# Attention in half-chunks of 64 tokens with two states per unit, and joint TensorE groups in one double-bank tile

## The chip, the cores and the metric

The kernel runs on one core of a Trainium2 chip. The metric is the device time of one execution in microseconds. TensorE (PE) does the matmuls, VectorE (DVE), ScalarE (ACT) and GpSimd (POOL) work beside it, and SyncE (SP) issues most transfers. Each engine runs its own instructions in program order and waits for others on semaphores. Matmul results land in PSUM, in banks of 512 f32 per partition, from where DVE or ACT must fetch them.

## What is computed

A linear attention with decay, whose output goes through a squared-ReLU feed-forward network (FFN). The inputs are random; the attention's are f32, the FFN's weights f64.

```python
B, H, S, D = 4, 8, 768, 48                # batch, heads, tokens, head size
state = zeros(B, H, D, D)
for t in range(S):
    y[:, :, t] = r_t @ (state + (u * k_t) v_t^T)
    state = w_t[:, :, :, None] * state + k_t v_t^T      # decay per key channel
x = y.transpose(0, 2, 1, 3).reshape(3072, 384)
h = relu(x @ w_in)                        # w_in 384 x 2048
out = (h * h) @ w_out                     # w_out 2048 x 384
```

## The kernel before

The tokens are cut into NC = 6 chunks of C = 128. A unit is one chunk of one batch entry: 24 units, numbered 4c + b, each with 8 heads in NP = 4 pairs. A pair's two heads lie on partitions 0 to 47 and 64 to 111 (J = 64, HP = 112); Q = 64 is half a chunk. Inside a chunk the decay is folded into the keys and queries by running products (DVE scans, L630, and the steps up to L653), so that a unit needs only matmuls.

A unit of chunks 1 to 5 has these steps on PE, f32 and packed four at a time into quarters of the array:

- scores (L693), keys times queries, into two PSUM tiles `mts`; DVE puts them through the causal mask into two SBUF tiles `Ms` (L696), whose diagonal blocks ACT has filled before (`diag`, L680);
- `past`: the old state times the queries (`inter`, L715), 8 matmuls of 128 columns, and the turned keys (`across`, L720), 4 transposes of the whole array; ACT copies the keys to SBUF (L739);
- `mix`: masked scores times values (`part`, L728), added to the same PSUM, and the outer products of keys and values (`outer`, L747), which DVE adds to the state (L809) and POOL multiplies with the chunk's decay (L812).

Then ACT and DVE write the unit's output as a high and a low part (L789, L790) into `xT`, and SP sends six small transfers per two units that put the fourth head pair in place (L797). In chunk 5 no state is kept, so `across` and `outer` fall away. Chunk 0 has no old state and an order of its own.

All PSUM steps of attention take their tiles from the pool `a`, two banks. The FFN has two banks `hp` and four accumulators `ob`. One FFN step multiplies the weights of 128 hidden columns with a chunk's x (L832, 9 matmuls of 512 columns into an hp bank), squares through L837, L838, L840, L841 (ACT, DVE, ACT, DVE) and multiplies with the second weights (L847, 12 matmuls of 384 columns). Chunk 0 runs its first 6, chunk 1 all 16 steps in two half-width parts (`HALF`), so that they can begin when two units are done. The weights come in 8 groups of 1.5 MB, each of which ACT, DVE and POOL split into two f32r parts.

The order on every engine is made by a planner (`Plan`): each step has a cost, its dependencies, and a rank out of a table (`Ranks`); the planner simulates the engines and writes down the order. A step marked with `mode` is one that packs the array. Where it expects PE to idle early on, it puts filler transposes (L888). SP's order of loads comes from the same tables.

Of the kernel before, what the change touches and what calls it, by code (L numbers as in the profile page):

```python
# [35 lines left out]
class Plan:  # L36
# [949 lines left out]
```

## Time and profile before

| | before |
|---|---|
| three runs, us | 546.95, 547.07, 545.52 (median 546.95) |
| profiled execution, its own time | 545.76 us |
| its span | 543.9 us |
| granted TensorE clock | 0.996 |
| PE busy | 526.4 us (97%) |
| DVE / ACT / POOL busy | 367.1 / 281.8 / 101.4 us |

The span runs from the first to the last instruction; the execution's own time is 1.9 us longer. A busy PE is not a PE at its peak, since matmuls overlap: how long a step holds PE is read from one step's start to the next step's start. In a row, `a<-pt,S` says that a tile a was written from pt and S; `x32` counts rows, and an f32 matmul has two rows, an FFN matmul (f32r) and a transpose one.

### The profile page before, as it was taken

Reading aid. Unit: us, or ns where it says so; the run is one execution under the profiler, and the core shown is the slowest. Engines: PE = TensorE matmul, PEld = TensorE weight load, DVE = VectorE, ACT = ScalarE, POOL = GpSimd, SP = SyncE. Lnnn points to the kernel's source line nnn. Section 1 sums busy time; section 2 is a strip of 40 time slices with the busy share of each in tenths; the row PEclk is TensorE's granted clock in tenths of the full one; section 3 lists DMA queues with packets and bytes.
Section 4 is the critical chain, followed back from the end, with each engine's and each line's share of the span. In section 5 each row is a group of like instructions: output and inputs, shape, how many; then the busy total and the mean of one; then the engine's idle time right before and its main releaser. Section 6 shows DMA issues by size and latency. Waiting matters only on the chain.

```text
span 543.9 us, 12917 instructions
## 1 busy us (share of the span) xinstructions
PE 526.4 (97%) x5047; PEld 465.7 (86%) x5047; DVE 367.1 (67%) x770; ACT 281.8 (52%) x730; POOL 101.4 (19%) x121
## 2 busy tenths in 40 slices
PE   8899989999999999999999999999999999999995
PEld 8788978878999889988888888889888989899894
DVE  6889899989969596498859597875653233433331
ACT  3668568486664747356465757526433222432321
POOL 5344543144303021030301203020000000000000
PEclk9999999999999999999999999999999999999998
DMA  9979988666483745747256565644002000000001
GB/s 161 175 183 227 244 173 195 151 109 136 93 151 72 138 91 101 140 92 134 48 97 122 101 125 117 129 91 84 1 6 68 16 1 1 29 32 0 1 1 61
DMA packets 222978, 53.01 MB, mean 97 GB/s; under 512 B 212672, under 2 KB 217792, under 8 KB 222912
## 3 DMA queue, kind: packets, MB, share of 16 engines
q1 hardware_dynamic: 220016, 50.75, 46.6%
q10 hardware_dynamic: 2896, 1.38, 1.0%
q8 instruction: 42, 0.69, 0.6%
q14 instruction: 24, 0.20, 0.1%
HBM read 31.65 MB, written 4.72 MB: 67 GB/s over the span
## 4 chain that ended last, share of the span: by engine, by line
PE 77%; DMA 10%; DVE 4%; ACT 3%; SPq 3%; issue 1%; POOL 0%; ACTq 0%; DVEq 0%
PE hp L832 33%; PE ob L847 32%; DMA ri<-in_moe_w_in_dram 4%; DMA v<-in_v_dram 3%; PE a L693 3%; PE a L728 3%; DMA st<-in_w_dram 2%; PE a L715 2%; SPq L572 2%; PE a L720 1%; PE a L747 1%; ACT m L680 1%; SPq L605 1%; DVE g L841 1%; DVE pt L630 1%
## 5 line engine op out<-in xcount | busy, mean ns | idle before, releaser
L847 PE MATMUL ob<-wo,g 128*128 128x384 f32 x1152 | 223.4, 340 | 1.4 <-DVE g L841 1.4
L832 PE MATMUL hp<-x,wi 128*128 128x512 f32 (+1 forms) x1062 | 219.9, 355 | 3.4 <-DVE g L841 3.2
L847 PEld LDWEIGHTS ob<-wo,g 128*128 128x128 f32 x1152 | 198.9, 188 | 7.7 <-DVE g L841 2.2
L832 PEld LDWEIGHTS hp<-x,wi 128*128 128x128 f32 x1062 | 173.1, 188 | 32.8 <-DVE g L841 6.8
L838 DVE SCALAR_TENSOR_TENSOR hp<-hp,t 128x512 f32<-128x512 f32 (+1 forms) x118 | 69.8, 593 | 91.3 <-ACT t L837 90.8
L837 ACT ACTIVATE t<-hp 128x512 f32<-128x512 f32 (+1 forms) x118 | 61.1, 518 | 118.5 <-PE hp L832 64.2
L841 DVE TENSOR_TENSOR g<-hp,g 128x512 fp32r<-128x512 f32 (+1 forms) x118 | 68.9, 585 | 32.3 <-ACT g L840 31.6
L840 ACT CAST g<-hp 128x512 fp32r<-128x512 f32 (+1 forms) x118 | 59.7, 506 | 51.9 <-DVE hp L838 51.5
L680 ACT ACTIVATE m<-diag,beta 128x64 f32<-128x64 f32 x192 | 50.0, 340 | 11.6 <-DVE beta L668 7.3
L660 POOL TENSOR_TENSOR st<-st 128x384 f32<-128x384 f32 x24 | 24.3, 1017 | 65.6 <-DVE st L581 58.4
L630 DVE TENSOR_TENSOR_SCAN pt<-pt,zero 112x128 f32<-112x128 f32 x80 | 29.0, 412 | 1.7 <-DMA st<-in_w_dram 1.7
L790 DVE SCALAR_TENSOR_TENSOR x<-a,x 112x128 fp32r<-112x128 f32 (+2 forms) x68 | 20.2, 329 | 12.2 <-ACT x L789 10.9
L696 DVE COPY_PREDICATED m<-caus,a 128x384 f32<-128x384 uint8 x48 | 25.9, 584 | 3.1 <-PE a L693 2.9
L662 POOL TENSOR_TENSOR st<-st,un 128x384 f32<-128x384 f32 x24 | 27.3, 1141 | 1.6
L581 DVE STREAM_TRANSPOSE st<-st 128x1152 f32<-128x1152 f32 x20 | 27.0, 1361 | 0.0
L728 PEld LDWEIGHTS a<-m,v 64*48 64x48 f32 (+1 forms) x768 | 20.5, 126 | 7.3 <-issue 4.1
L637 ACT ACTIVATE m<-pt 112x512 f32<-112x512 f32 x24 | 15.2, 631 | 22.3 <-DVE pt L630 19.4
L693 PEld LDWEIGHTS a<-pt 48*64 48x64 f32 x768 | 19.2, 133 | 7.8 <-ACT m L680 1.6
L789 ACT ACTIVATE x<-a 112x128 fp32r<-112x128 f32 (+2 forms) x68 | 18.1, 313 | 14.1 <-PE a L747 7.0
L728 PE MATMUL a<-m,v 64*48 64x64 f32 (+3 forms) x768 | 24.8, 250 | 0.4 <-DVE m L696 0.4
L693 PE MATMUL a<-pt 48*64 48x128 f32 (+1 forms) x768 | 22.8, 250 | 1.4 <-DVE pt L653 1.4
L812 POOL TENSOR_TENSOR S<-S,Ec 112x192 f32<-112x192 f32 x16 | 8.1, 508 | 82.8 <-DVE S L809 82.8
(86 smaller groups left out, 441.8 us busy)
## 6 DMA issues: line engine op xcount, KB each, us to landing
pt<-st SPq DMA_DIRECT2D x120, 96.0 KB, 2.3
ro<-in_moe_w_out_dram SPq DMA_DIRECT2D x8, 768.0 KB, 7.4
v<-in_v_dram SPq DMA_DIRECT2D x88, 48.0 KB, 2.5
st<-in_w_dram SPq DMA_DIRECT2D x11, 384.0 KB, 4.4
st<-in_k_dram SPq DMA_DIRECT2D x11, 384.0 KB, 5.7
st<-in_r_dram SPq DMA_DIRECT2D x11, 384.0 KB, 5.7
out_dram<-q SPq DMA_DIRECT2D x20, 192.0 KB, 2.1
ri<-in_moe_w_in_dram SPq DMA_DIRECT2D x8, 384.0 KB, 6.4
```

Source lines behind the costliest of these rows:

```text
L581: V.transpose(out=zt[:, i].rearrange("a t p q i -> a t (p q) i"), in_=sv[:, :, i].rearrange("s t p q x -> s t (p q) x"))
L630: lambda p=p: V.tensor_tensor_scan(out=pt[:, 0, p], data0=src(0)[:, p], data1=zero.broadcast_to([HP, C]), initial=1.0, op0=ALU.mult, op1=A ...
L662: P.add("pool", 0.97, rank("rk"), lambda: G.tensor_tensor(out=rk(), in0=rk(), in1=un.rearrange("s (h d) -> s h d", d=D), op=ALU.mult), w=[ ...
L680: A.activation(Ms[j].tile[:, mo(p, y):mo(p, y) + Q], diag2, AF.Copy, scale=beta.tile[:, i:i + 1])
L693: T.matmul(mts[j].tile[q * Q:q * Q + Q, o:o + C - y * Q], kq[js, g:g + Q], pt[js, 1, 2 * q + p, y * Q:], start=True, stop=True, skip_group ...
L728: T.matmul(spot(p)[to:to + n + D, y * Q:], vt.tile[qs, o - n:o + D], Ms[j].tile[qs, mo(p, y):mo(p, y) + C - y * Q], start=(c == 0 and p == ...
L832: T.matmul(hp.tile[:, 0:n], wi[f][:, wl, kt], xT[:, kt, xl, xs], start=(m == 0), stop=(m == 3 * KT - 1))
L837: P.add("act", 0.49 if full else 0.28, rank("g"), lambda: A.activation(t(), h(), AF.Relu), r=[hp], w=[(g, 1)])
L838: P.add("dve", 0.6 if full else 0.33, rank("g"), lambda: V.scalar_tensor_tensor(out=h(), in0=h(), scalar=0.0, in1=t(), op0=ALU.max, op1=AL ...
L840: P.add("act", 0.48 if full else 0.26, rank("g"), lambda: A.copy(out=hi(), in_=h()), r=[hp], w=[(g, 0)])
L841: P.add("dve", 0.6 if full else 0.33, rank("g"), lambda: V.tensor_tensor(out=lo(), in0=h(), in1=hi().bitcast(F32), op=ALU.subtract), r=[hp ...
L847: T.matmul(obs[b][:, 0:DM], g.tile[0][:, gl, o:o + C], wo[f][:, wl], start=(f == 0 and m == 0), stop=(f == NF - 1 and m == 2))
```

## The change

Chunks 1 to 5 get another attention (chunk 0 keeps its own, with a fixed order of the fetches from one bank).

- The pool `a` is now the two halves of one tile `ab` of 1024 columns. From chunk 1 on both halves belong to a fixed layout: for each head pair 128 columns of output (`Y`) and 128 columns of a zone that holds either outer products or scores.
- Scores, mix and old-state products are computed within halves of 64 tokens. For that a unit has two states: `S[b]` at its start, and `S1` = `S[b]` + outer products of its first half. The second half's queries meet `S1`. `S2` = `S1` + outer products of the second half is decayed by POOL into the next `S[b]`. So the matmuls are 16 of 64 columns each for `inter`, `mix` and `scores`, and 16 of 48 for `outer` (8 in chunk 5).
- The keys are turned earlier, in a step of its own (L717) between FFN matmuls, into a bank of the pool `hp`; one ACT copy of 448 columns takes them.
- PE's packed work is done in two groups per unit. `advance(k)` joins `inter` of unit k with `outer` of unit k + 1, and `mix` of unit k with `scores` of unit k + 1.
- One mask of 512 columns (L780) in place of two of 384; `Ms` becomes one tile `M`; x is fetched in two pieces instead of three; POOL copies the decay in three pieces.
- Keys of the form `(sl, "bank")` put ACT's fetch of x, DVE's mask and DVE's fetch of x in that order.
- All ranks are new, some of the planner's costs differ, and the pool `m` has six tiles instead of seven.

```diff
-    LANES, RUNS, SLACK, START = 8, 2300, 1.0, 3.6
+    LANES, RUNS, SLACK, START = 8, 2300, 1.0, 4.0
     UNITS = (
-        (-1354.91, -1161.61, 40.98, ...
+        (-1377.03, -1144.15, -483.17, ...
-    pas = [ps_a.tile([128, 512], F32, name=f"a{i}") for i in range(2)]
+    ab = ps_a.tile([128, 1024], F32, name="ab")
+    pas = [ab[:, i * 512:i * 512 + 512] for i in range(2)]
+            M, Kt, kp = Slot("m", unit), Slot("m", unit), Slot("hp")
+            P.add("pe", 0.2 * ys, rank("ktp"), turned_k, r=KK, w=[kp])
+            P.add("act", 0.03 + 0.2 * ys, rank("kt"), lambda: A.copy(out=Kt.tile[:, 0:2 * ys * HP], in_=kp.tile[:, 0:2 * ys * HP]), r=[kp], w=[Kt])
+            def outer():
+                for p in range(2):
+                    for y in range(ys):
+                        for j in range(2):
+                            for q in range(2):
...
+            def inter():
+                for h, t in enumerate((lambda: Ss[b], lambda: S1.tile)):
+                    for p1 in range(2):
+                        for j in range(2):
+                            for q in range(2):
+                                p = 2 * q + p1
+                                js, n, to, o = slice(j * J, j * J + D), ahead(p, j), side(p, j) * J, PC + block(p, j) * D
+                                T.matmul(ab[to:to + n + D, p * 2 * C + h * Q:p * 2 * C + h * Q + Q], t()[js, o - n:o + D], pt[js, 1, p, h * Q:h * Q + Q],
+                                         start=(h == 0 and p1 == 0), stop=False, skip_group_check=True)
...
+                P.add("dve", 0.27, rank("S"), lambda: V.tensor_tensor(out=sv(S1.tile), in0=zone(0, D)[0:HP], in1=sv(Ss[b]), op=ALU.add), r=["dS", ("S", b)], w=[S1])
+                    P.add("dve", 0.27, rank("S"), lambda: V.tensor_tensor(out=sv(S2.tile, 0), in0=zone(J, D)[0:HP], in1=sv(S1.tile), op=ALU.add), r=["dS", S1], w=[S2])
+                    P.add("pool", 0.46, rank("S"), lambda: G.tensor_tensor(out=Sd, in0=S2.tile..., in1=Eb(), op=ALU.mult), r=[S2, Ec], w=[("S", b)])
+                P.add("dve", 0.6, rank("mask"), lambda: V.copy_predicated(out=mv(), mask=..., data=zone(0, C)...), r=["scores"], w=[M, ("Y", "bank")])
...
+    def advance(k):
+        a, z = (stages[i] if 0 <= i < len(stages) else None for i in (k, k + 1))
+        if a:
+            fns, r, w, cost = fns + [a["inter"]], r + a["r2"], w + ["Y"], cost + 0.45
+        if z:
+            fns, r, w, cost = fns + [z["outer"]], r + z["r1"], w + ["dS", "scores"], cost + z["outer_cost"]
+        P.add("pe", cost, (a or z)["rank"]("past"), lambda fns=fns: group(fns), r=r, w=w + AB, mode=1, claim=[a["x3"]] if a else [], after=turns)
...
+        if a:
+            fns, r, w, cost = fns + [a["mix"]], r + a["r4"] + ([] if z else ["past"]), w + ["Y"], cost + 0.45
+        if z:
+            fns, r, w, cost = fns + [z["scores"]], r + z["r3"], w + ["dS", "scores"], cost + 0.45
+        P.add("pe", cost, (a or z)["rank"]("mix"), lambda fns=fns: group(fns), r=r, w=w + AB, mode=1, claim=[z["M"]] if z else [])
```

How it moves instructions, at two places. First PE in chunk 1 before the change: the old state's group of one unit, between FFN matmuls (pt are queries and keys, S the state, st and v inputs, m the SBUF tiles of masked scores and keys).

```order
L832 MATMUL hp_146<-x_135,wi_81 128x256 x9
L715 MATMUL a_147<-pt_129,S_132 64x128
L715 MATMUL a_147<-pt_129,S_132 48x128
L715 MATMUL a_148<-pt_129,S_132 48x128
L715 MATMUL a_148<-pt_129,S_132 64x128
L715 MATMUL a_147<-pt_129,S_132 64x128
L715 MATMUL a_147<-pt_129,S_132 48x128
L715 MATMUL a_148<-pt_129,S_132 48x128
L715 MATMUL a_148<-pt_129,S_132 64x128
L720 MATMUL a_147<-ident,pt_129 128x112 x2
L720 MATMUL a_148<-ident,pt_129 128x112 x2
L847 MATMUL ob_141<-wo_79,g_95 128x384 x3
```

After it, PE in chunk 2: the group that joins the two half-chunk products of one unit (with the state S_132 and the middle state S_166) to the outer products of the next one, of which the first two rows are shown:

```order
L742 MATMUL ab<-pt_129,S_132 64x64
L742 MATMUL ab<-pt_129,S_132 48x64 x2
L742 MATMUL ab<-pt_129,S_132 64x64 x2
L742 MATMUL ab<-pt_129,S_132 48x64 x2
L742 MATMUL ab<-pt_129,S_132 64x64
L742 MATMUL ab<-pt_129,S_166 64x64
L742 MATMUL ab<-pt_129,S_166 48x64 x2
L742 MATMUL ab<-pt_129,S_166 64x64 x2
L742 MATMUL ab<-pt_129,S_166 48x64 x2
L742 MATMUL ab<-pt_129,S_166 64x64
L731 MATMUL ab<-v_152,m_159 64x48 x2
L731 MATMUL ab<-v_152,m_159 48x48 x2
```

and, a little later, the group that joins mix and scores:

```order
L936 MATMUL hp_146<-x_136,wi_65 128x512 x9
L761 MATMUL ab<-m_155,v_154 64x64
L761 MATMUL ab<-m_155,v_154 48x64 x2
L761 MATMUL ab<-m_155,v_154 64x64 x2
L761 MATMUL ab<-m_155,v_154 48x64 x2
L761 MATMUL ab<-m_155,v_154 64x64 x2
L761 MATMUL ab<-m_155,v_154 48x64 x2
L761 MATMUL ab<-m_155,v_154 64x64 x2
L761 MATMUL ab<-m_155,v_154 48x64 x2
L761 MATMUL ab<-m_155,v_154 64x64
L751 MATMUL ab<-pt_130 64x64 x16
L936 MATMUL hp_145<-x_136,wi_69 128x512 x9
```

The transposes of the keys (L720, right behind L715) have left the packed group; three visits to the packed array per unit have become two.

The second place is SP near the start, before the change: weight groups 3 and 4 (ri_68, ro_70 and ri_76, ro_78), chunk 1's values v and its raw inputs st.

```order
L519 DMA ri_68<-in_moe_w_in_dram 16x3x512 x2
L521 DMA ro_70<-in_moe_w_out_dram 128x2x768
L605 DMA v_153<-in_v_dram 64x4x48 x4
L605 DMA v_154<-in_v_dram 64x4x48 x4
L572 DMA st_151<-in_w_dram 128x16x48
L572 DMA st_151<-in_k_dram 128x16x48
L572 DMA st_151<-in_r_dram 128x16x48
L519 DMA ri_76<-in_moe_w_in_dram 96x2x512
L519 DMA ri_76<-in_moe_w_in_dram 48x512 x2
L519 DMA ri_76<-in_moe_w_in_dram 16x3x512 x2
L521 DMA ro_78<-in_moe_w_out_dram 128x2x768
L519 DMA ri_72<-in_moe_w_in_dram 96x2x512
```

After it:

```order
L608 DMA v_94<-in_v_dram 64x4x48 x2
L575 DMA st_150<-in_w_dram 128x16x48
L575 DMA st_150<-in_k_dram 128x16x48
L575 DMA st_150<-in_r_dram 128x16x48
L522 DMA ri_68<-in_moe_w_in_dram 96x2x512
L522 DMA ri_68<-in_moe_w_in_dram 48x512 x2
L522 DMA ri_68<-in_moe_w_in_dram 16x3x512 x2
L524 DMA ro_70<-in_moe_w_out_dram 128x2x768
L522 DMA ri_76<-in_moe_w_in_dram 96x2x512
L522 DMA ri_76<-in_moe_w_in_dram 48x512 x2
L522 DMA ri_76<-in_moe_w_in_dram 16x3x512 x2
L524 DMA ro_78<-in_moe_w_out_dram 128x2x768
```

The raw inputs of chunk 1 stand ahead of weight group 3, its values have gone behind group 5, and of group 5 only the first piece still stands ahead of the transfers that spread the turned inputs (pt), which stood behind all of it.

More of the change, by code (lines that the diff above doesn't have):

```diff
@@ L468 @@
     P.pool("v0", first_v)
-    P.pool("m", [at.tile([128, NP * C], F32, name=f"m{i}") for i in range(7)])
+    P.pool("m", [at.tile([128, NP * C], F32, name=f"m{i}") for i in range(6)])
     P.pool("ly", last_y)
@@ L472 @@
     P.pool("Ec", [at.tile([HP, NP, 1], F32, name=f"Ec{i}") for i in range(4)])
+    P.pool("S1", [at.tile([HP, PC + NP * D], F32, name=f"S1{i}") for i in range(1)])
+    P.pool("S2", [at.tile([HP, NP * D], F32, name=f"S2{i}") for i in range(2)])
     P.pool("beta", [at.tile([128, H + H // 2], F32, name=f"beta{i}") for i in range(4)])
@@ L663, in attention, with halves @@
         s1, s2, h1, h2 = slice(0, Q), slice(Q, C), slice(0, H // 2), slice(H // 2, H)
[L665 to L666 removed]
+        P.add("dve", 0.46, rank("beta"), lambda: V.tensor_reduce(out=beta.tile[:, 0:H], in_=rk(), axis=AX.X, op=ALU.add), r=[(st, ui, 1)], w=[beta], port=True)
+        def halves():
             V.tensor_tensor(out=beta.tile[s1, H:], in0=beta.tile[s2, h1], in1=beta.tile[s2, h1], op=ALU.max)
@@ L669, in sums @@
             V.tensor_tensor(out=beta.tile[s1, h2], in0=beta.tile[s1, H:], in1=beta.tile[s1, H:], op=ALU.max)
-        P.add("dve", 1.04, rank("beta"), sums, r=[(st, ui, 1)], w=[beta], port=True)
+        P.add("dve", 0.58, rank("beta"), halves, w=[beta], port=True)
+        block = lambda p, j: 2 * (p // 2 ^ j) + p % 2
+        side = lambda p, j: 1 - j if p in ACROSS else j
+        ahead = lambda p, j: PC if side(p, j) == 0 else 0
+        xT = xTs[c % 2]
+        cs = slice(b * C, b * C + C)
@@ L801, in attention @@
[L801 to L812 removed]
+        ly = Slot("ly")
@@ new lines, in between @@
+        def between():
+            for q in range(KT):
+                T.matmul(spot(TILES[q]), sel[:, q], ly.tile, start=(q in (0, 2)), stop=False, skip_group_check=True)
+            across()
+            part(TILES)
+        P.add("pe", 0.34, rank("mix"), lambda: part([SPLIT]), r=[*VK, *Ms], w=[(far_yb, 3)], mode=3, claim=[yb, ly, Kt])
+        P.add("act", 0.14, rank("mix"), lambda: A.copy(out=ly.tile, in_=spot(SPLIT)[0:HP]), r=[(far_yb, 3)], w=[ly])
+        P.add("pe", 1.82, rank("mix"), between, r=[*VK, *Ms, *KK, ly], w=[*both_yb, *KW], mode=3, more=14 if b == 1 else 0)
@@ new lines, in evacuate @@
+        def evacuate():
+            for i, t in enumerate(both_yb):
+                P.add("act", 0.24, rank("kt"), lambda i=i, t=t: A.copy(out=kv(Kt, i * 2 * HP, None), in_=kv(t, 2 * C, None)), r=[(t, "kt")], w=[(Kt, i), (t, "bank")])
+        moves([("x", yb, lambda: ybv()[:, 0:2], lambda: xT[:, 0:2, 0, cs], lambda: xT[:, 0:2, 1, cs], xk + (0,), 0.28, 0.33),
+               ("x", far_yb, lambda: ybv(far_yb)[:, 0], lambda: xT[:, 2, 0, cs], lambda: xT[:, 2, 1, cs], xk + (1,), 0.16, 0.205)], evacuate)
@@ new lines, in attention, with state @@
+        P.add("pe", 0.46, rank("dS"), outer, r=[*VK, (Kt, 0), (Kt, 1)], w=[*both_yb, *KW], mode=3, more=-10 if b == 1 else 0)
+        for i, t in enumerate(both_yb):
+            def state(i=i, t=t):
+                ps = slice(2 * i, 2 * i + 2)
+                V.tensor_tensor(out=Sd[:, ps], in0=t.tile[0:HP, 2 * C:2 * C + 2 * D].rearrange("a (p e) -> a p e", p=2), in1=Eb()[:, ps], op=ALU.mult)
+            P.add("dve", 0.165, rank("S"), state, r=[(t, "dS"), Ec], w=[("S", b)])
+    stages = []
@@ new lines, with group @@
+    AB = [Slot("a") for _ in range(2)]
+    def advance(k):
+        a, z = (stages[i] if 0 <= i < len(stages) else None for i in (k, k + 1))
+        turns = []
+        if k < 0:
+            turns = [s for s in P.steps if any(x.pool == "a" for x in s.slots)]
+        def group(fns):
+            for fn in fns:
+                fn()
+        fns, r, w, cost = [], [], [], 0.0
+        if a:
[4 more added lines that the diff above has]
+        if a:
+            a["after_inter"]()
+        if z:
+            z["after_outer"]()
+        else:
+            P.add("act", 0.06, a["rank"]("S"), lambda: A.copy(out=nothing, in_=ab.rearrange("a (k x) -> a k x", k=2)[0:HP, :, 0]), r=["Y"], w=["past"])
+        fns, r, w, cost = [], [], [], 0.0
+        if a:
+            fns, r, w, cost = fns + [a["mix"]], r + a["r4"] + ([] if z else ["past"]), w + ["Y"], cost + 0.45
+        if z:
+            fns, r, w, cost = fns + [z["scores"]], r + z["r3"], w + ["dS", "scores"], cost + 0.45
+        P.add("pe", cost, (a or z)["rank"]("mix"), lambda fns=fns: group(fns), r=r, w=w + AB, mode=1, claim=[z["M"]] if z else [])
+        mask = z["after_scores"] if z else lambda: None
+        if a:
+            a["after_mix"](mask)
+        else:
+            mask()
@@ L834, in ffn @@
         full = n == 512
-        P.add("pe", 2.075 if full else 1.07, rank("hp"), first, r=wkeys("wi") + [x for b in range(*bs) for x in xkeys(c, b)], w=[hp])
+        P.add("pe", 2.085 if full else 1.075, rank("hp"), first, r=wkeys("wi") + [x for b in range(*bs) for x in xkeys(c, b)], w=[hp])
         hi, lo, t, h = (lambda: g.tile[0][:, 0, 0:n]), (lambda: g.tile[0][:, 1, 0:n]), (lambda: g.tile[1][:, 0:n]), (lambda: hp.tile[:, 0:n])
@@ L867 @@
     for c in range(NC):
-        if c:
-            for b in range(B):
-                attention(c, b, lambda nm, c=c, b=b: RANKS.unit(c, b, nm))
+        for i in range(c * B + 1 if c else B, c * B + B + 1):
+            if i < NC * B:
+                attention(i // B, i % B, lambda nm, i=i: RANKS.unit(i // B, i % B, nm))
+            advance(i - B - 1)
         order = [(f, bs) for bs in ((0, 2), (2, B)) for f in range(HALF[c])] + [(f, (0, B)) for f in range(HALF[c], NF)]
```

437 lines of the change are left out of this document (222 added, 215 removed), and 48 rows, old and new, of the table UNITS.

## The prediction

> **What bounds the kernel now.** I read the page first, then busy time by stretches, then the chain, then TensorE's timeline around the attention steps.
>
> ```profile
> span 543.9 us, 12917 instructions
> PE 526.4 (97%) x5047; PEld 465.7 (86%) x5047; DVE 367.1 (67%) x770; ACT 281.8 (52%) x730; POOL 101.4 (19%) x121
> PE 77%; DMA 10%; DVE 4%; ACT 3%; SPq 3%; issue 1%; POOL 0%; ACTq 0%; DVEq 0%
> ...
> 60.00:80.00 20.00, 17.32 (x162) 15.85 (x161) 17.55 (x31) 10.98 (x27) 12.03 (x8) 1.00 0.93 221
> 80.00:100.00 20.00, 20.00 (x127) 17.52 (x127) 18.52 (x36) 16.87 (x40) 4.76 (x4) 1.00 0.89 191
> 100.00:120.00 20.00, 19.27 (x210) 15.98 (x208) 18.34 (x33) 11.40 (x34) 7.68 (x7) 1.00 0.54 112
> 120.00:140.00 20.00, 19.82 (x209) 17.72 (x209) 19.20 (x38) 12.47 (x27) 7.00 (x7) 1.00 0.54 113
> ```
>
> TensorE is busy 97% of the span at the full granted clock (1.00), and the chain is 77% PE. In the stretches of 20 us the columns are PE, weight loads, DVE, ACT and POOL busy, granted clock, DMA share and GB/s. The first 80 us are another stage: DMA is at 0.93 there, and part of PE's busy time is filler transposes. From 80 us on PE hardly pauses, so an attention matmul saved after that point is time saved, as long as its step still comes when PE wants it. Up to 140 us VectorE is nearly full too (18.5, 18.3 and 19.2 of 20 us): there its work decides with PE's.
>
> Busy times of pipelined matmuls overlap, so I price steps by the distance from one start to the next. One unit of chunks 1 to 4, from the timeline of PE:
>
> ```profile
> 301.60 0.67 PE L715 MATMUL a<-pt,S 48*64 48x128 f32 x16
> 302.19 0.60 PE L720 MATMUL a<-ident,pt 112*128 112x112 f32 x4
> 302.56 2.31 PE L832 MATMUL hp<-x,wi 128*128 128x512 f32 x9
> 304.81 0.90 PE L728 MATMUL a<-m,v 64*64 64x128 f32 x32
> 305.51 0.65 PE L747 MATMUL a<-v,m 64*48 64x48 f32 x32
> 306.09 2.31 PE L832 MATMUL hp<-x,wi 128*128 128x512 f32 x9
> ...
> 309.30 2.33 PE L847 MATMUL ob<-wo,g 128*128 128x384 f32 x12
> 311.56 0.96 PE L728 MATMUL a<-m,v 64*64 64x128 f32 x26
> ...
> 323.45 0.90 PE L693 MATMUL a<-pt 48*64 48x128 f32 x32
> 324.28 0.98 PE L832 MATMUL hp<-x,wi 128*128 128x512 f32 x3
> ```
>
> The scores group (L693) takes 324.28 - 323.45 = 0.83 us; the group of old-state products and turned keys (L715, L720) 302.56 - 301.60 = 0.96; the mix with the outer products (L728, L747) 306.09 - 304.81 = 1.28, of which L747 is 0.58. The trace counts each f32 matmul twice (16 in the program are x32 here), since it runs in two passes.
>
> What a group costs around itself shows in the FFN run beside it. From the chain, undisturbed:
>
> ```profile
> 473.78 4.16 PE hp L832 x18
> 477.94 5.22 PE ob L847 x30
> ```
>
> Nine hp matmuls take 2.08 and twelve ob matmuls 12 x 5.22/30 = 2.09. Between two attention groups the nine took 304.81 - 302.56 = 2.25 and the twelve 311.56 - 309.30 = 2.26: 0.17 us for each group, half of it going in and half coming out. So a unit costs PE 0.83 + 0.96 + 1.28 + 3 x 0.17 = 3.58 us.
>
> The last chunk, which keeps no state, gives the price by width:
>
> ```profile
> 401.87 0.67 PE L715 MATMUL a<-pt,S 48*64 48x128 f32 x16
> 402.47 0.79 PE L847 MATMUL ob<-wo,g 128*128 128x384 f32 x3
> 403.19 0.90 PE L728 MATMUL a<-m,v 64*64 64x128 f32 x32
> 404.02 3.42 PE L847 MATMUL ob<-wo,g 128*128 128x384 f32 x18
> ```
>
> L715 is sixteen rows of 128 columns: 0.60 us with the way out. L728 is sixteen of 128 and sixteen of 64: 0.83. So sixteen rows of 64 columns cost 0.23. L728 alone took 305.51 - 304.81 = 0.70 where L747 followed it and 0.83 here, so the way out is 0.13, and sixteen rows of 128 columns cost 0.60 - 0.13 = 0.47, twice the 0.23. A unit of the last chunk costs 0.83 + 0.60 + 0.83 + 3 x 0.17 = 2.77.
>
> **The change, part by part.** *Matmuls.* Each of old state, scores and mix becomes 16 matmuls (x32 rows) of 64 columns: 2 x 0.23 = 0.46 each. The outer products stay 16 of 48 columns: 0.58 - 0.13 = 0.45. The transposes of the keys leave the packed group and stand between FFN matmuls; the nearest row is eight transposes there:
>
> ```profile
> 42.59 1.04 PE L618 MATMUL a<-ident,st 128*128 128x128 f32 x8
> 43.39 0.72 PE L832 MATMUL hp<-x,wi 128*128 128x256 f32 x4
> ```
>
> That is 0.80/2 = 0.40 for four; with a little for the first FFN matmul behind them I take 0.45 (bounds 0.37, from L720, and 0.40 + 0.17, if they pay like a group).
>
> *Groups.* Three per unit become two: the old-state products of one unit with the outer products of the next (0.46 + 0.45 + 0.13 = 1.04), and the mix of one with the scores of the next (0.46 + 0.46 + 0.13 = 1.05). With 2 x 0.17 and 0.45 that is 2.88 against 3.58: 0.70 less, 11.2 us over 16 units. The last chunk turns half the keys (0.25) and has half the outer products (0.23), so 0.25 + 0.82 + 1.05 + 0.34 = 2.46 against 2.77: 0.31 less, 1.2 us over four. The pipeline has 21 pairs of groups for 20 units: one pair more, 2 x (0.13 + 0.17) = 0.6. PE's sum: 11.2 + 1.2 - 0.6 = 11.8 us less.
>
> *Other engines.*
>
> ```profile
> L696 DVE COPY_PREDICATED m<-caus,a 128x384 f32<-128x384 uint8 x48 | 25.9, 584 | 3.1 <-PE a L693 2.9
> ```
>
> DVE's two masks of 384 columns (1.17 us a unit) become one of 512, 0.58 to 0.78; the corrections of x are two instead of three, the state sums two as before. About half a microsecond of DVE a unit goes. ACT has one key copy instead of two, and POOL three small decay copies instead of one, on an engine that is 19% busy. All this lies beside PE's FFN work after 140 us, and I cost it at nothing; if the cover goes, PE waits for a masked tile, which is the last rival below. DMA bytes and the FFN's instructions stay as they are.
>
> *The start.* The tables also reorder the loads on SP. Ahead of weight group 4 the eight v transfers of chunk 1 go back and chunk 1's w, k and r come before group 3.
>
> ```profile
> 43.90 8.91 DMA v<-in_v_dram
> 53.37 1.63 SPq L572
> ...
> 57.66 5.37 DMA ri<-in_moe_w_in_dram
> ...
> 80.79 4.13 PE hp L832 x18
> ```
>
> On the chain these v transfers hold 8.9 us and the three loads 57.66 - 53.37 = 4.3; the first 512-wide hp step, with which PE's steady stretch begins, runs at 80.8. A gain from the new order ends where DVE is full: 60 - 56.1 = 3.9 us of its time were free between 80 and 140. A loss is group 3 behind the loads, 4.3. I take a gain of 1, a little on the side of the longer row, and keep -4 to +4.
>
> Sum against the profiled execution: its time is 545.8 us for a span of 543.9; 545.8 - 11.8 - 1 = 533.0. The median of the three runs shown, 546.95, lies 1.2 above it, inside the range below.
>
> **Rivals.** *(a) The start gives more.* If the earlier weights let DVE use all its free time from 60 us on, 3.9 + 2.4 = 6.3, it ends at 545.8 - 11.8 - 6.3 = 527.7. For it: PE, too, idles 20 - 17.32 = 2.7 us between 60 and 80. Against it: what DVE must do ahead of chunk 0's last FFN step is the same work as before.
>
> *(b) The turned keys take an FFN bank.* They now land in one of the two hp banks. From the page:
>
> ```profile
> L837 ACT ACTIVATE t<-hp 128x512 f32<-128x512 f32 (+1 forms) x118 | 61.1, 518 | 118.5 <-PE hp L832 64.2
> L838 DVE SCALAR_TENSOR_TENSOR hp<-hp,t 128x512 f32<-128x512 f32 (+1 forms) x118 | 69.8, 593 | 91.3 <-ACT t L837 90.8
> L840 ACT CAST g<-hp 128x512 fp32r<-128x512 f32 (+1 forms) x118 | 59.7, 506 | 51.9 <-DVE hp L838 51.5
> L841 DVE TENSOR_TENSOR g<-hp,g 128x512 fp32r<-128x512 f32 (+1 forms) x118 | 68.9, 585 | 32.3 <-ACT g L840 31.6
> ```
>
> An FFN step holds its bank for 2.08 us of matmuls and 2.20 of these four, with hops some 4.8; two banks and steps 4.17 apart offer 8.3. The keys need 0.40, a copy of 448 columns, a little under L840's 0.51 for 512, and perhaps one L837 or L840 ahead of it: 1.4. That fits into 3.5 free microseconds at full width. In the half-width steps of chunk 1 the slots are half as long and it may not. If eight of the twenty key turns cost 1.2 us each, 9.6 of the 12.8 are gone: 542 to 543. If each of the twenty cost over 0.64, nothing is left.
>
> *(c) Slower: one double bank in a row.* Every attention group now writes the same double-bank tile, so the next group waits until ACT and DVE have emptied it: after the mix two ACT copies (mean 0.31, L789), a mask of about 0.7 and two DVE corrections (0.33, L790), some 2.0 us; after the outer products two sums, about 0.6. If PE stood still for all of it, 21 x 2.6 = 55 us would come on top and the run end near 588. It decides from 12.8/55 = 23% of that, 0.3 us per group.
>
> ```profile
> L790 DVE SCALAR_TENSOR_TENSOR x<-a,x 112x128 fp32r<-112x128 f32 (+2 forms) x68 | 20.2, 329 | 12.2 <-ACT x L789 10.9
> L789 ACT ACTIVATE x<-a 112x128 fp32r<-112x128 f32 (+2 forms) x68 | 18.1, 313 | 14.1 <-PE a L747 7.0
> ...
> PE a L715 <- DVE m L696: 0.7, 1, 0.7
> PE a L747 <- ACT m L739: 0.4, 1, 0.4
> PE a L728 <- DVE m L696: 0.4, 1, 0.4
> ```
>
> Against it: before, each group takes both tiles of the same pool as well, and PE waited for their emptying three times, 1.5 us in all, since FFN matmuls stand between groups. The Trainium skill (Perfetto Trace Analysis, Matmuls) speaks against this change: independent matmul groups should rotate through PSUM banks so that one is emptied while the next one runs. By that rule taken alone the time is this rival's; the three waits just shown do not bear it out here, because the FFN, not the next attention group, is what runs meanwhile.
>
> *(d) No change.* The step saves as told, but chunk 1 is held by DVE and its steps come late, so that 11 or more of the 12.8 us come back as waits between 80 and 240 us: 544 to 547. DVE has half a microsecond less per unit, which speaks against it.
>
> **How the numbers follow.** The forecast, PE's sum carried through with small waits, 528 to 539: 0.62. (a) below 528: 0.12. (b) 539 to 545: 0.16. (d) 0.04. (c) or (b) beyond its break-even, above 548: 0.06. Each is a clear gain but the last two, so faster 0.90, same 0.04, slower 0.06, with 0.3% (1.6 us) as about what a measurement of this kernel can tell from no change. The range 525.5 to 542 leaves out the far part of (a), about 0.05, and of (b) what lies above 542, with (c) and (d) about 0.15. The forecast's own range is 528 to 539.
>
> **What would show it.** After 140 us the old-state, scores and mix groups should each have x32 rows of 64 columns at 0.46, the two joint groups 1.04 and 1.05 from start to start, and FFN runs between them be 0.17 longer. If the 64-column rows come at the pace of the 128-column ones, the width step is wrong. Waits of hp matmuls for the key copy show (b), waits of the joint groups for x, the mask or the state sums show (c), and the first 512-wide hp step, before or after 80.8 us, shows the start's share. The likeliest error is a few waits of a microsecond each where the new order expects a step sooner than it comes.

## The result: slower by 1.6%

The changed kernel took 554.43 us (median of 4 runs, 553.50 to 556.90) against 546.24 us (545.31 to 547.07) for the kernel before, a ratio of 1.0158 with a 95% interval of 1.0118 to 1.0197. The forecast was 533.0 us, so it had the wrong sign. The profiled execution took 554.14 us, with a span of 552.1.

### The profile page after: what moved, and what is told of

It reads as the page before. It is cut to its first block, busy times and chain, and to the rows that moved or that the text cites. A ratio compares the mean times of both kernels' runs of the same rounds, so it can differ in the third digit from the quotient of the medians.

```text
span 552.1 us, 13615 instructions
## 1 busy us (share of the span) xinstructions
PE 517.5 (94%) x5435; PEld 463.6 (84%) x5435; DVE 364.7 (66%) x735; ACT 281.3 (51%) x691; POOL 110.6 (20%) x161
## 4 chain that ended last, share of the span: by engine, by line
PE 64%; DVE 9%; ACT 4%; issue 2%; DMA 1%; POOL 0%; ACTq 0%; SPq 0%; DVEq 0%; POOLq 0%
PE hp L936 29%; PE ob L951 28%; PE ab L761 2%; PE ab L742 2%; PE ab L751 1%; DVE hp L942 1%; PE hp L717 1%; DVE g L945 1%; ACT m L712 1%; PE ab L731 1%; DMA x<-x 1%; ACT t L941 1%; DVE st L584 1%; DVE q L543 1%; ACT m L640 1%
## 5 line engine op out<-in xcount | busy, mean ns | idle before, releaser
L936 PE MATMUL hp<-x,wi 128*128 128x512 f32 (+1 forms) x1062 | 223.1, 359 | 12.2 <-DMA x<-x 8.1
L936 PEld LDWEIGHTS hp<-x,wi 128*128 128x128 f32 x1062 | 176.3, 192 | 40.3 <-issue 8.2
L941 ACT ACTIVATE t<-hp 128x512 f32<-128x512 f32 (+1 forms) x118 | 60.7, 516 | 135.6 <-PE hp L936 107.8
L712 ACT ACTIVATE m<-diag,beta 128x64 f32<-128x64 f32 x160 | 40.4, 338 | 12.0 <-DVE beta L676 12.0
L650 POOL COPY Ec<-pt 64x4 f32<-64x4 f32 x20 | 6.7, 333 | 120.4 <-DVE pt L633 107.4
L584 DVE STREAM_TRANSPOSE st<-st 128x1152 f32<-128x1152 f32 x20 | 26.6, 1354 | 0.0
L640 ACT ACTIVATE m<-pt 112x512 f32<-112x512 f32 x24 | 15.2, 631 | 20.6 <-DVE pt L633 17.1
L694 ACT ACTIVATE x<-ab 112x384 fp32r<-112x384 f32 (+3 forms) x48 | 16.5, 374 | 17.0 <-PE ab L751 12.8
L556 POOL TENSOR_TENSOR wi<-q,wi 128x768 fp32r<-128x768 f32 x8 | 16.4, 2050 | 27.8 <-ACT wi L555 13.5
L780 DVE COPY_PREDICATED m<-caus,ab 128x512 f32<-128x512 uint8 x20 | 14.6, 732 | 5.9 <-ACT x L694 5.8
L697 DVE SCALAR_TENSOR_TENSOR x<-ab,x 112x384 fp32r<-112x384 f32 (+3 forms) x48 | 18.1, 399 | 0.3 <-ACT m L871 0.3
L556 POOL TENSOR_TENSOR wo<-q,wo 128x768 fp32r<-128x768 f32 x8 | 14.9, 1865 | 16.3 <-ACT wo L555 16.2
L654 DVE TENSOR_TENSOR pt<-pt,m 112x512 f32<-112x512 f32 x24 | 17.0, 714 | 1.1 <-ACT m L641 0.7
```

The source lines that it names most:

```text
L556: P.add("pool", 1.78, rank, lambda q=q, tt=tt: G.tensor_tensor(out=tt[:, 1], in0=q.tile, in1=tt[:, 0].bitcast(F32), op=ALU.subtract), r=[q ...
L584: V.transpose(out=zt[:, i].rearrange("a t p q i -> a t (p q) i"), in_=sv[:, :, i].rearrange("s t p q x -> s t (p q) x"))
L712: A.activation(M.tile[:, o:o + Q], diag2, AF.Copy, scale=beta.tile[:, i:i + 1])
L936: T.matmul(hp.tile[:, 0:n], wi[f][:, wl, kt], xT[:, kt, xl, xs], start=(m == 0), stop=(m == 3 * KT - 1))
L941: P.add("act", 0.49 if full else 0.28, rank("g"), lambda: A.activation(t(), h(), AF.Relu), r=[hp], w=[(g, 1)])
```

## The profile after

The head of the page of the changed kernel, with the chain's shares by engine:

```profile
span 552.1 us, 13615 instructions
PE 517.5 (94%) x5435; PEld 463.6 (84%) x5435; DVE 364.7 (66%) x735; ACT 281.3 (51%) x691; POOL 110.6 (20%) x161
...
PE 64%; DVE 9%; ACT 4%; issue 2%; DMA 1%; POOL 0%; ACTq 0%; SPq 0%; DVEq 0%; POOLq 0%
```

TensorE is busy 8.9 us less than before (526.4); 11.8 were forecast. But it now idles 552.1 - 517.5 = 34.6 us where it idled 17.5: 17.1 more. The difference, 17.1 - 8.9 = 8.2, is the loss in the span. The chain's share of VectorE went from 4% to 9%, and PE's from 77% to 64%. Busy time by stretches tells where PE idles. After (columns as before: PE, weight loads, DVE, ACT, POOL, granted clock, DMA share, GB/s):

```profile
120.00:140.00 20.00, 17.53 (x126) 15.66 (x130) 19.37 (x36) 13.27 (x33) 5.22 (x9) 0.91 0.56 111
140.00:160.00 20.00, 10.32 (x151) 9.68 (x142) 8.67 (x25) 7.08 (x23) 4.13 (x5) 0.74 0.53 104
```

and before, in the second of them:

```profile
140.00:160.00 20.00, 19.58 (x284) 18.04 (x283) 14.79 (x44) 14.47 (x49) 5.40 (x7) 1.00 0.65 126
```

Between 140 and 160 us PE works half the time (10.32 of 20, before 19.58), at a granted clock of 0.74 instead of 1.00. Note that VectorE is not busy there either (8.67): no engine is full there, so a chain of latencies is running. Of the 17.1 us more of idle time 11.5 lie between 120 and 160 us: PE works 27.85 of these 40 us, and worked 39.40 before (19.82, in the row of the prediction, and 19.58). A second, smaller part lies between 200 and 240 us, where PE is busy for 36.28 us after and 39.68 before. The timeline of PE around the first part:

```profile
132.25 6.38 PE L951 MATMUL ob<-wo,g 128*128 128x384 f32 x24 [1.96 <-ACT g L944]
...
139.34 0.69 PE L742 MATMUL ab<-pt,S 48*64 48x64 f32 x32
...
141.56 0.70 PE L761 MATMUL ab<-m,v 64*64 64x64 f32 x32 [1.07 <-DVE S L772]
...
150.86 3.71 PE L936 MATMUL hp<-x,wi 128*128 128x256 f32 x18 [8.14 <-DMA x<-x]
```

Chunk 0's last FFN step ends at about 138.5, then come one pair's turned keys and its two joint groups, and then nothing for 8.14 us, until the transfers of x have landed and chunk 1's first half-width FFN step may start, at 150.86. Before, the same step began right behind chunk 0's last:

```profile
128.47 5.39 PE L847 MATMUL ob<-wo,g 128*128 128x384 f32 x30
133.69 2.31 PE L832 MATMUL hp<-x,wi 128*128 128x256 f32 x18
```

The chain of the changed kernel shows whom the step waited for; the pieces are start, length, what:

```profile
107.81 2.61 DVE st L584 x2
...
133.52 0.66 DVE pt L644 x2
...
137.64 0.68 DVE pt L660
138.32 1.30 DVE st L584
...
142.79 0.67 ACT x L694 x2
...
144.21 0.45 DVE x L697
...
148.78 1.99 DMA x<-x
150.86 3.73 PE hp L936 x18
```

Read it backwards. The FFN of chunk 1's first half needs x of units 4 and 5. Unit 5's x (L694, L697) is written after the group `mix` of unit 5, which the change joins with `scores` of unit 6, and the group ahead of it joins `past` of unit 5 with `outer` of unit 6. So x of unit 5 waits for unit 6's keys and queries: their block transposes on DVE (L584, at 107.8), sixteen transfers on SP, scans, and the products of L644 to L660. Those of unit 6 end at 137.7 and those of unit 7 at 138.3; the turned keys of both stand ahead of the joint group in PE's order. Units are prepared two at a time, so units 6 and 7 are the next pair, and belong to chunk 1's second half. Before, neither unit of the first half had anything to do with unit 6. The x of the later one, there unit 4, was written at 124, by VectorE's timeline, and the next pair was prepared at the same time as now:

```profile
124.02 0.61 DVE L790 SCALAR_TENSOR_TENSOR x<-a,x 112x256 fp32r<-112x256 f32 x2
...
138.41 2.63 DVE L581 STREAM_TRANSPOSE st<-st 128x1152 f32<-128x1152 f32 x2
```

The transposes of units 8 and 9, that follow the preparation of 6 and 7, start at 138.41 before and at 138.25 after. The pace of the pairs is what it was (107.79 to 138.25, 30.5 us a pair). What is new is that chunk 1 stands behind the second pair instead of the first.

The hole itself is not the pair's preparation alone. The last joint group ends at 142.7 and x of unit 5 is in place at 145.4 (VectorE's row of 0.28 us at 145.14). Then SP's timeline shows where x waits:

```profile
140.94 5.81 SPq L594 DMA_DIRECT2D pt<-st  x7
146.86 3.78 SPq L793 DMA_DIRECT2D x<-x  x6
```

Seven transfers of units 8 and 9 stand ahead of the six sends, which begin 1.4 us after x is ready; from there it takes 4.0 us until PE starts. The 1.07 us between the two joint groups also have the transposes of units 8 and 9 in them (VectorE, 138.25 to 140.9), behind which the sums stand. So up to some 2 us of the idle time, by these rows, come from the order of the rows of units 8 and 9. Before, the sends started at 126.1 and their landing was covered by chunk 0's FFN, which ran until 133.7.

## The experiments

Three theories stood for what costs the time. **The join**: chunk 1's first half waits for the next pair's preparation. **VectorE**: what holds it is VectorE's load, 18 to 19 of 20 us up to 140 us. **The clock**: the hole halves TensorE's clock, and the slow matmuls behind it are the loss. (Letters in an expectation hold for that expectation.) Most kernels below have the same steps as one of the two kernels, with the order on every engine written out as a list in place of the planner's:

```diff
     def order(self):
+        if len(self.steps) > 500:
+            return self.written()
```

### e3: the kernel before, with the wait alone

Nothing of the change is in it. In the list, `mix` of unit 4 (in the kernel before the second unit of the first half), its corrections, its state sums and the sends of x stand behind the key products of unit 6, as they do in the changed kernel; seven steps of unit 7 follow them.

> The kernel before (546.2 us), with nothing of the change in it but the wait: the mix of unit 4, the last one that chunk 1's first FFN half needs, stands behind unit 6's prepared keys on VectorE, and its x and transfers behind it; unit 7's v loads and diagonal and one buffer of unit 6 are moved so that this can be; nothing else is. Theory A: this alone makes the hole: PE waits 6 to 10 us before the first half-width hp step, which comes at 140 to 144 us instead of 133.7, and the run takes 553 to 559. If the loss came from something else in the change (the keys in an hp bank, the one double bank, the clock), it costs under 3 us: 546 to 549.

It took 553.98 us (552.78 to 557.24) against 545.43: ratio 1.0147 [1.0130, 1.0164], 8.5 us more, with the TensorE work of the kernel before. Its PE timeline:

```profile
136.79 0.65 PE L853 MATMUL a<-v,m 64*48 64x48 f32 x32
142.79 4.18 PE L938 MATMUL hp<-x,wi 128*128 128x256 f32 x18 [5.35 <-DMA x<-x]
```

A shorter pause (5.35 us, in the change 8.14) with the same releaser appears, and 18 slow matmuls behind it. So moving this wait alone costs the kernel before 8.5 us, as much as the change's net loss of 8.2. It is not the whole miss: had PE's 11.8 us and the 1 us of the start been saved as forecast, the wait would have left the change some 4 us faster. The rest is below. This profiled execution (557.24) is also the longest of the six. In it the first 512-wide FFN step comes at 83.29 instead of 80.62, before any of the moved steps, at a granted clock of 0.50 between 50 and 55 us; the price of 8.5 us goes by the medians.

### e1 and e2: the one pair taken apart

e1 runs the groups of unit 5 and of unit 6 one after the other instead of together, and moves the rows from about 118 us on to suit. e2 keeps the joint groups and moves the same rows.

```diff
+    APART = (1,)
...
+        if k in APART and a and z:
+            move(k, a, None)
+            move(k, None, z)
+        else:
+            move(k, a, z)
```

> The changed kernel with one joint pair taken apart: unit 5's old-state products and mix are groups of their own, and unit 6's outer products and scores follow as another pair. The rows between about 118 and 165 us are put in a new order for it; all others stand as in the changed kernel (554.4 us; the kernel before 546.2). Theory A (the join): unit 5's tokens are late because their matmuls stand in one group with unit 6's, whose keys and queries VectorE prepares last. Then the first half-width hp step comes at 135 to 142 us instead of 150.9 and the run takes 543 to 549. Theory B (the order, not the join): no more is gained than in the next kernel, where the same rows are reordered and the pair stays joined. Theory D (the transfers of x alone hold the step): the hole stays, 552 to 555.

> The changed kernel with all pairs joined as they are, and the same rows, about 118 to 165 us, in a new order. Theory A: unit 6's preparation still has to come first, the first half-width hp step stays at 147 us or later, and the run takes 552 to 555. Theory B: the order alone gives most of it back, 543 to 549, as taking the pair apart does.

e1 took 555.51 (555.37 to 556.76), ratio 1.0192 [1.0175, 1.0210]; e2 559.84 (557.01 to 561.22), ratio 1.0274 [1.0250, 1.0297]; before was at 545.43. In e1 the 8-us hole is gone, but the time did not follow:

```profile
142.72 1.23 PE L1053 MATMUL hp<-x,wi 128*128 128x256 f32 x9
...
146.88 0.60 PE L822 MATMUL hp<-ident,pt 112*128 112x112 f32 x4 [2.41 <-DVE pt L765]
```

Chunk 1 starts 8 us sooner (142.72), with no idle time of its own, and then PE waits for the keys of unit 7 (L822, 2.41; unit 6's were turned at 139.60), and again at later pairs. The largest new wait is 3.22 us, ahead of L849 at 128.99: there unit 5's own group waits until unit 4's x has left the double bank. So the hole at chunk 1 goes with the join, but undoing one join does not bring its price back: waits appear at the next places that need the pair or the bank. This experiment missed what it was to show in the total. Its first 40 us also ran some 3 us later than those of the changed kernel, at a granted clock of 0.52 between 25 and 30 us and 0.80 between 30 and 35 (the changed kernel: 1.00 from 25 to 30), so its total says less than its trace. e2, with the joint groups kept, moved the hole into smaller waits at the same place (2.24, 1.44, 3.39 and 1.80 us by its timeline) and lost 4 us more: moving rows by computed times alone made it worse. Its time lies above what either theory gave, and since the two written orders differ, the 4.3 us between e1 and e2 are only an indication of what the join costs.

### e5, e6, e7: the same search for all

All three have their whole order from one and the same search by computed times: e5 the changed kernel, e6 with pairs 5|6 and 7|8 taken apart, e7 the kernel before. Their filler transposes write into banks in use, so part of the output is overwritten; the work is the same.

> The changed kernel, all pairs joined, with the order of all its rows written anew (steps and buffers as they are; a search that favours orders which survive late steps). Theory B (the loss is the order that the tables gave): the saved 11.8 us of matmuls come through, 536 to 543. Theory A (in the stage that VectorE bounds a joined unit waits for the next unit's preparation, whatever the order): 545 to 553, with PE idle for 6 us or more between 120 and 240 us.

> The same rewriting of all rows, with the pairs of units 5|6 and 7|8 (the two that close a half of chunk 1) taken apart; two more groups' way in and out, 1.2 us. Theory A: 3 to 8 us below the joined one of this call. Theory B: 0 to 2 us above it.

> The kernel before with its rows written anew in the same way, so that the two kernels are compared under one kind of order. Theory A: it lies 5 us or more below the joined one of this call, since its units do not wait for each other. Theory B: 5 us or more above it, since its matmuls cost 11.8 us more.

They took 558.91 (554.51 to 564.47), 551.83 (549.55 to 553.63) and 549.95 (548.17 to 551.02) against 546.05: ratios 1.0240 [1.0163, 1.0317], 1.0096 [1.0065, 1.0127] and 1.0071 [1.0044, 1.0098]. The joined order is the slowest, as the join would have it; e6 and e7 are not told apart, since their intervals overlap. The 9.0 us between e5 and e7 is near the 8.2 that separate the two kernels under their own orders, but e5's four runs spread over 10 us, and without its longest (564.47) the distance is 5.4. So the loss does not hang on one unlucky table of ranks, but its size here is uncertain. e5 lies above the ranges of both its theories, and in its trace no wait between 40 and 280 us is longer than 2.8 us while PE idles 33.5 us of the span: the joined order loses by many small waits too. The rewritten orders of the two kernels were worse than the planner's (e5 against 554.43, e7 against 546.05).

### e4: fillers that keep the clock up

```diff
-    IDLE = (110.0, 4.0, 0.3, 0.12)
+    IDLE = (150.0, 4.0, 0.3, 0.12)
```

This lets the planner put filler transposes into idle time up to 150 us.

> The changed kernel with filler transposes in PE's pauses up to 150 us instead of 110: 98 more, 81 of them in the hole ahead of chunk 1's first half-width hp step. Theory C (part of the loss is the clock: granted 0.50 after the pause, and the first 18 half-width hp matmuls take 3.7 us instead of 2.2): these take 2.1 to 2.3 and the run 551 to 553. If the clock costs nothing: 553.5 to 555.5. The hole itself stays under every theory; should the fillers run past the end of the wait, up to 1 us is lost.

It took 555.80 (554.48 to 558.48), ratio 1.0208 [1.0179, 1.0236], no better than the change alone. PE's timeline in it:

```profile
143.60 9.06 PE L992 MATMUL hp<-ident 128*128 128x128 f32 x81
152.42 2.40 PE L936 MATMUL hp<-x,wi 128*128 128x256 f32 x18
```

The 18 matmuls now take 2.40 us instead of 3.71, but start 1.56 later, since the fillers ran past the arrival of x. 1.3 won, 1.6 lost. So the clock behind the hole is not the cause; it is at most 1.3 us of it. The slow stretch at 132 us, ahead of the hole, was not changed by this.

### e8 and e9: VectorE lightened

The changed kernel (e8) and the kernel before (e9) leave out the sign and the low bits in the split of the FFN weights. That takes 32 VectorE instructions away, some 28 us.

```diff
-                V.scalar_tensor_tensor(out=qi, in0=bits[:, :, 1], scalar=0x80000000, in1=qi, ...
+                return
```

> The changed kernel without two of VectorE's three instructions in each split of a weight group (the sign and the low bits; L543 and L548, 32 instructions of 0.87 us, some 28 us of VectorE between 25 and 127 us; the weights are then not the reference's). All rows stand in the same order. Theory A (a joined unit waits for the next unit's preparation because VectorE is full): with VectorE free the hole goes, the first half-width hp step comes at 128 to 138 us instead of 150.9, and the kernel lies 4 to 12 us below the next one of this call, as the sum of the matmuls said. If the loss is not VectorE's (the keys in an hp bank, the one double bank, the transfers of x): it stays 5 to 10 us above the next one.

> The kernel before with the same 32 instructions left out (L540 and L545), rows in the same order. Its PE hardly waits from 80 us on, so little can be gained there; the start may come sooner. Both theories: 535 to 546. It is the measure for the one above.

e8 took 552.23 (549.27 to 554.14), ratio 1.0110 [1.0064, 1.0156], e9 541.94 (540.92 to 542.18), ratio 0.9921 [0.9897, 0.9946], both to 546.2. The kernel before gained 4.3 us, the changed one 2.2, and the distance is 10.3 us instead of 8.2, the same within the intervals. If VectorE's load were the cause, it would have shrunk. From e8's timelines, first PE and then DVE:

```profile
147.01 5.61 PE L934 MATMUL hp<-x,wi 128*128 128x256 f32 x27 [8.21 <-DMA x<-x]
```

```profile
105.33 2.63 DVE L582 STREAM_TRANSPOSE st<-st 128x1152 f32<-128x1152 f32 x2
...
123.10 2.62 DVE L631 TENSOR_TENSOR_SCAN pt<-pt,zero 112x128 f32<-112x128 f32 x8
...
133.12 1.28 DVE L658 TENSOR_TENSOR pt<-pt,m 112x512 f32<-112x512 f32 x2
```

The hole is as long as before (8.21). From the transposes to the last key product the pair still takes 134.4 - 105.3 = 29 us, of which SP's sixteen transfers are 11.8. VectorE is less full meanwhile (14.32 of 20 us between 100 and 120, 17.18 between 120 and 140), and chunk 1 starts 3.9 us sooner (147.01). So with the planner's order kept, VectorE's load is not what makes the hole.

### e10 to e14: the next pair's steps moved forward

e10 is e8 with a written list: the scans and products of units 6 and 7 come up to where their operands are ready, and the transposes and transfers of units 8 and 9 move behind the sends of x. e11 is the same list for the whole weights, e12 is e1 with the weights of e8.

```
e10: scans of 6 and 7 ahead of the mask of 5; logarithms and key products ahead of FFN step 28
     turned keys, sums, joint group, x, sends ahead of chunk 0's last ob steps
     transposes, transfers and beta of 8 and 9 behind the sends
```

> The changed kernel without the sign and low bits of the split weights (as e8), its order written out and moved in one place: the steps of units 6 and 7 that stand ahead of chunk 1's first half (scans, logarithms, the differences, the three key products, the turned keys, the sums, the joint group, x, the sends) come up in the lists as soon as their operands can be there, and unit 8's transposes and its transfers on the SP queue stand behind the sends. e8 had its first half-width hp at 147.0 us and took 552.2. Theory A (what holds chunk 1 is the row of latencies of the next pair, and VectorE has room here): the scans move from 123.1 to about 120, the key products end at 130 and not 134.4, the sends start at 137 and not 143; first half-width hp at 139 to 141, time 545 to 548. Theory B (chunk 1 is held by something else that comes with the joint groups): hp stays within 2 us of 147, time 550 to 553.

> The same moved order with the whole weights, that is the changed kernel with nothing but these rows moved. Theory A with a full VectorE: VectorE has hardly 2 us free between 94 and 138 us, so the key products come no sooner than about 137; only unit 8's transposes (2.6 us) and the seven transfers ahead of the sends (5.8 us) are out of the way; first half-width hp at 145 to 148 against 150.9, time 549 to 552 against 554.4. If VectorE's load does not matter, it gains what e10 gains over e8: hp at 142 to 144, time 546 to 548. Theory B: 553 to 556.

> e1's kernel (the pair 5 with 6 taken apart) without the sign and low bits of the weights. Theory A: with the next pair's steps out of the way of chunk 1 and room on VectorE, what e1 gave back later (3.2 us for x, 2.4 for the turned keys, 1.1 and 1.3) is not lost: 537 to 543, at or below the 541.9 of the kernel before with the same weights (e9). Theory B (the joint order costs elsewhere as well, whatever VectorE carries): within 3 us of e8, 549 to 555.

They took 558.95 (556.03 to 562.61), 567.66 (565.76 to 569.13) and 550.36 (546.96 to 551.27) against 545.27: ratios 1.0272 [1.0227, 1.0316], 1.0418 [1.0394, 1.0442] and 1.0080 [1.0058, 1.0103]. In e10 chunk 1 began 5.5 us sooner than in e8, close to what theory A expected; then PE's timeline shows a new wait, and ACT's shows its source:

```profile
141.53 3.88 PE L1037 MATMUL hp<-x,wi 128*128 128x256 f32 x18 [2.42 <-DMA x<-x]
156.88 3.86 PE L1037 MATMUL hp<-x,wi 128*128 128x256 f32 x18 [11.47 <-DVE g L1046]
```

```profile
154.23 0.98 ACT L1061 COPY q<-ob 128x384 f32<-128x384 f32 x2 [7.57 <-DMA out_dram<-q]
```

The stores of chunk 0's output stood behind fifteen transfers of units 8 and 9 on SP's queue, ACT waited for them with a copy, and the FFN's squares were queued behind that copy. This wait was made by my list, so the totals of e10 and e11, which lie above both theories' times, do not decide between them. e11 has the same wait (11.20 us); its chunk 1 starts at 150.72, no sooner than in the change and 9.2 us later than in e10. So with whole weights VectorE's load does stand in the way of a better order there. e12 at 550.36 lies with its theory B (549 to 555), not with A (537 to 543): taking one pair apart does not bring the PE saving through even when VectorE has room. The first row of its list of PE's waits (total, times, longest) says where it stays:

```profile
PE hp L820 <- DVE pt L763: 5.0, 4, 2.4
```

Four times PE stands for the keys of a pair to be turned. So the hole at chunk 1 is the largest place at which the new arrangement waits for a pair's preparation, and not the only one.

e13 (light) and e14 (whole weights) put the stores ahead of the transfers.

> e10 with one thing moved: the last two copies and stores of chunk 0's output stand ahead of unit 8's transfers on the SP queue (in e10 they stood behind 15 of them, ScalarE could not go on without the stores, and PE stood 11.5 us behind ScalarE). Theory A (the row of latencies of the next pair is what holds chunk 1 when VectorE has room): first half-width hp at 141.5 as in e10, no wait of over 2 us in the 20 us behind it, time 546 to 549 against 552.2 of e8. Theory B (what the hole loses is lost behind it in any case, since the attention of the later pairs is what is late): hp at 141.5, the sum of the later waits larger by 5 us or more, time 551 to 554.

> e11 with the same move, whole weights. e11 had its first half-width hp at 150.7, no sooner than the changed kernel's 150.9, since VectorE was busy to 138 us in both, and then the 11.2-us wait behind the stores. Theory A with a full VectorE: hp at 150 to 151, the 11.2-us wait gone, 555 to 558 (567.7 less 11), that is no better than the changed kernel's 554.4 for a moved order. Theory B says the same here; what tells is whether any order of these rows reaches hp below 148: 551 or less would say that VectorE's load is no bound either.

They took 562.22 (560.26 to 563.61) and 570.31 (568.46 to 572.13) against 545.0: ratios 1.0315 [1.0277, 1.0353] and 1.0451 [1.0404, 1.0498], both far outside what either theory gave. e13's PE timeline:

```profile
143.64 4.14 PE L1037 MATMUL hp<-x,wi 128*128 128x256 f32 x18 [2.45 <-DMA x<-x]
153.12 4.21 PE L1037 MATMUL hp<-x,wi 128*128 128x256 f32 x18 [5.33 <-DVE g L1046]
...
165.60 0.45 PE L832 MATMUL ab<-v,m 64*64 64x48 f32 x2 [2.84 <-DMA v<-in_v_dram]
```

Now ACT holds the FFN up with steps of units 8 and 9 that stand ahead of its copies (5.33), and v of the next pair holds the joint groups up (2.84): its loads stand behind sixteen transfers of units 8 and 9 on SP and start 9 us later than in e8 (162.92 against 153.68). With the lightened weights the start of chunk 1 can be had sooner by 3.4 to 5.5 us than in e8, but in none of these lists did the total follow; with the whole ones it came no sooner (150.72 in e11, 152.75 in e14). Whether some list would keep the gain is open.

## Why the prediction was wrong, step by step

**PE's sum was right in its groups.** The joint groups, forecast at 1.04 and 1.05 from start to start, in the timeline of PE around 300 us:

```profile
301.80 0.69 PE L742 MATMUL ab<-pt,S 48*64 48x64 f32 x32
302.29 0.66 PE L731 MATMUL ab<-v,m 64*48 64x48 f32 x32
302.88 2.35 PE L951 MATMUL ob<-wo,g 128*128 128x384 f32 x12
...
307.25 0.70 PE L761 MATMUL ab<-m,v 64*64 64x64 f32 x32
...
308.34 2.33 PE L936 MATMUL hp<-x,wi 128*128 128x512 f32 x9
```

They are 302.88 - 301.80 = 1.08 and 308.34 - 307.25 = 1.09, and the x32 rows of 64 columns 0.49 where 0.46 was forecast; the FFN run between the two groups took 307.25 - 302.88 = 4.37 us, 0.20 longer than undisturbed (2.08 + 2.09), where 0.17 was forecast. Busy time fell by 8.9 us against 11.8, so 2.9 are missing; the slow clock accounts for about that, 24 matmuls in 6.38 us at 132.25 (30 took 5.39 before, so 2.1 more) and 18 in 3.71 at 150.86 (2.31 before, 1.4 more), together some 3.5.

**The step that failed is "All this lies beside PE's FFN work after 140 us, and I cost it at nothing".** Between 138 and 151 us there is no FFN work to lie beside: chunk 0's is done, and chunk 1's is what waits. The step priced a joint group by its matmuls and left out that a joint group starts when the later of its two units is ready. The condition was in the prediction, "as long as its step still comes when PE wants it", but got no price. The measured price: 8.1 us of idle PE at that place, and 1.4 of slow matmuls behind it. The other 2.1 follow the pause of 1.96 us ahead of 132.25, where chunk 0's last squares stood behind the scans of units 6 and 7 on VectorE (128.0 to 130.6). e3 measures the moved wait alone, added to the kernel before, at 8.5 us of run time.

The rest of the new idle time is in the list of PE's waits between 40 and 280 us (total, times, longest):

```profile
PE hp L936 <- DMA x<-x: 8.1, 1, 8.1
...
PE ob L951 <- ACT g L944: 2.7, 2, 2.0
PE ab L761 <- DVE S L772: 1.8, 2, 1.1
PE hp L717 <- DVE g L945: 1.6, 1, 1.6
PE ab L856 <- DVE x L697: 1.4, 1, 1.4
PE hp L717 <- DVE pt L660: 1.2, 2, 0.6
```

PE waits 2.8 us to turn keys and 2.7 for chunk 0's squares; the joint groups wait 1.8 for sums. The 1.4 for x (L856, at 39.81 us) belong to chunk 0's own attention and not to a joint group. These are of the kind that the prediction named as its likeliest error, "a few waits of a microsecond each", and with the hole they make 16.8 us. The kernel before waited 1.5 for its groups, by the rows of the prediction, and 1.4 for squares of chunk 0, at 79.81 us:

```profile
PE ob L847 <- DVE g L841: 1.4, 1, 1.4
```

That leaves 13.9 of the 17.1 us; the other 3 are spread over waits of a microsecond and less. The whole lists of waits sum to 27.7 us after and 11.1 before, and so account for 16.6 of the 17.1.

**The start** was to give 1 us. From the timeline of PE:

```profile
80.73 3.29 PE L936 MATMUL hp<-x,wi 128*128 128x256 f32 x18
```

This run holds nine half-width and nine full-width matmuls, so the first 512-wide step begins some 2.2 us before its end of 84.02, at 81.8 instead of 80.8. The start cost 1 us, within the bounds. In this stage the granted clock was 0.66 between 65 and 70 us (before: 1.00), behind a wait of 1.03 us at 63.2.

**The rivals.** (a), the start gives more: no. (b), the turned keys take an hp bank: one wait of 1.6 us in place of the 9.6 it needed. (c), one double bank in a row: the joint groups wait 1.8 us for sums and 0.4 for the mask, against the 12.8 from which it would have decided. The Trainium skill (Perfetto Trace Analysis, Matmuls), which asks for bank rotation, was thus not what decided here. In e1, where one pair was taken apart, the bank did cost 3.22 us at one place. (d), no change, comes nearest: it put the loss at chunk 1, as waits between 80 and 240 us, with chance 0.04 and 544 to 547 us. Its place was right. Its mechanism, chunk 1 held by VectorE, is not borne out with the planner's order (e8 and e9: the hole stays without 28 us of VectorE's work), and its price was 8 us short, since it let the wait eat the saving and no more.

## What to carry to other kernels

When two units' work is put into one group, price the group's start as well as its length: it comes with the later unit, and whatever was due after the earlier unit (here x, its transfers, and the next chunk's FFN) comes later by the distance of the two. Draw for the first use after each join what PE could do meanwhile; a cover that holds in the steady part may be missing at a chunk's border. A hole of that kind is seen in the trace as PE idle while no other engine is full, and it is tested by adding the wait alone to the old kernel.

## What the runs showed of the hardware

A pause of 1.96 us (ahead of 132.25) was followed by a granted clock of 0.84 between 132 and 134 us and 0.50 behind that; in stretches of 2 us of the changed kernel:

```profile
134.00:136.00 2.00, 2.00 (x8) 2.00 (x7) 2.00 (x5) 0.48 (x1) 0.00 (x0) 0.50 0.06 13
...
152.00:154.00 2.00, 2.00 (x12) 2.00 (x11) 0.42 (x1) 0.38 (x1) 0.00 (x0) 0.54 0.55 96
154.00:156.00 2.00, 1.65 (x14) 1.45 (x12) 0.96 (x4) 1.13 (x3) 0.00 (x0) 1.00 0.56 98
```

PE is busy throughout 134 to 136 and yet at 0.50; after the hole, work starts at 150.86 and the clock is back at about 153.8 (a mean of 0.54 over 152 to 154), some 3.0 us later. The Trainium skill (TensorE: Matmul & The Clock Gate, Part 1, What's actually happening) gives about 3.4 us of work for the way up, which the 3.0 measured here come near, and at least one idle window of about 3.4 us for the way down, which a pause of 1.96 us undercuts here. Shorter waits do not settle it either way: one of 1.03 us at 63.2 was followed by 0.66 between 65 and 70 us, one of 1.04 at 24.75 by no fall (1.00 from 25 to 30), and in the kernel before one of 1.36 ahead of 79.81 by none (1.00 from 80 on). So which of these waits brings the clock down is open.
